# Queries and keys in 1 KB packets, and five chunks' probabilities turned on TensorE, in a windowed-attention and SoLU kernel

## The chip, the cores and the metric

The kernel runs on one core of one Trainium2 chip. The metric is the device time of one execution in microseconds. A core has TensorE (PE in the rows; PEld is its weight load), VectorE (DVE), ScalarE (ACT), GpSimd (POOL) and SyncE (SP), which here issues every DMA. Matmul results land in PSUM, all other tiles lie in SBUF; "DRAM" below is the chip's large memory behind the DMA queues.

## What is computed

Attention with a window and sink keys, and behind it a two-layer network with a SoLU in between, all in float32 (the weights arrive as float64):

```python
# q, k, v: (4, 8, 768, 64); n_sink = 4, window = 128
scores = (1 / sqrt(64)) * q @ k.T
keep = (key < n_sink) | ((0 <= query - key) & (query - key < window))
a = softmax(where(keep, scores, -1e9))
x = (a @ v).transpose(0, 2, 1, 3).reshape(3072, 512)
h = x @ w_in                                   # w_in: (512, 1024)
solu = h * softmax(h)
ln = (solu - mean(solu)) / sqrt(var(solu) + 1e-6) * g_ln
out = ln @ w_out                               # w_out: (1024, 512)
```

## The kernel before

The 4 x 768 tokens are 24 chunks of 128. `places` numbers them: chunk 0 is the first of batch 0, chunk 1 the first of batch 1, chunks 2 to 6 the rest of batch 0, 7 to 11 the rest of batch 1, 12 to 17 batch 2, 18 to 23 batch 3. Each chunk goes through the same stages:

- *Loading.* Queries and keys of chunks 0 to 6 come one chunk at a time (line 470) and are turned by TensorE against an identity (`turn`, line 513), which ScalarE copies out of PSUM (544, 548). For the other chunks a whole batch comes at once, in four DMAs each for q and k (line 473); VectorE turns them in 32x32 blocks (`turn_q` 526, `turn_keys` 539; `again_k` turns chunk 1's keys anew). The tiles `qn` and `kn` of such a batch have one buffer, so the next batch can't come before the last transpose of this one.
- *Scores* (567, TensorE) into one of two pairs of PSUM banks (`banks`, handed out by `claim` and given back by `done`), `pick` (584), masks with the row minimum (597, VectorE), exponentials (606, ScalarE), the inverse of the row sums (611, 612).
- *Normalising* (617, GpSimd) into `pn`, which has one buffer.
- *Turning the probabilities.* `pn` is stored to DRAM (`pd`; lines 632, 634, 637), reloaded in four pieces (`pb`, 642), and turned by VectorE in 32x32 blocks into `pt` (`flip_p`, 647). For chunks that are not the first of their batch, GpSimd splits `pt` into the part for the own and the part for the previous chunk's values (655, 661); sinks go a way of their own (667 to 694).
- *Values* (704, TensorE), x split into a high and a low part (709 ScalarE, 713 VectorE), *hidden layer* (724, three matmuls per block: high by high, high by low, low by high), SoLU and norm (729 to 764), a store and reload of u through DRAM and a turn on VectorE (771 to 781; chunks 0, 1, 22 and 23 are turned by TensorE, 790), split (797, 801), *projection* (815), scaling (821), store (826).

The two weights are made ready in the first part of the run: 16 blocks (`wraw`, line 373) are fetched as float64 and split into high and low parts by ScalarE, VectorE and TensorE (385 to 428).

Each step (a function with a chunk and an index) has a number, and the table `ORDER` (lines 19 to 118) says in which order the steps are issued. Each engine, and SP's DMA queue, runs its own instructions in just that order, and waits at the head of its queue. So the table sets what stands in front of what on every engine.

The lines that load a batch, take its raw tile and turn it:

```python
src[b, 2 * i:2 * i + 2].rearrange("h (t p) d -> p (h t) d", p=32)                          # 473
st[nm + "n", b].rearrange("p (e t x) -> p e t x", e=2, x=D)[:, :, 4 * c:4 * c + 4]         # raw
nc.vector.transpose(t[:, 2 * e:2 * e + 2], raw(n, "q")[:, e].rearrange("p t (y x) -> p y t x", y=2))
```

So partition p gets every 32nd row of a head, a piece of 64 floats (256 bytes) each.

Of the kernel before, what the change touches and what calls it, by code (L numbers as in the profile page):

```python
# [122 lines left out]
BIT_TAGS = ("uh", "ul", "ob", "uh", "ul", "ob", "uh", "ul") * 2  # L123
P = 128
NPS = 12
NSK = 4
W2P = 4
SEG = 132
BLK = 68
HALF = 64  # L130
NEG = 8.0e9
EPS_SUM = 1e-9
EPS_LN = 1e-6


# [48 lines left out]
def _banded(ctx, tc, q, k, v, n_sink, window, w_in, w_out, g_ln, out, val, wts, wpool, consts):  # L184
# [320 lines left out]
    def raw(n, nm):  # L505
        b, c = place(n)
        return st[nm + "n", b].rearrange("p (e t x) -> p e t x", e=2, x=D)[:, :, 4 * c:4 * c + 4]
# [530 lines left out]
```

## Time and profile before

| | |
|---|---|
| median of 3 runs | 436.63 us (435.45 to 438.84) |
| the profiled execution, its own time | 437.73 us |
| its span in the trace | 436.0 us |
| TensorE busy | 393.3 us (90%) |
| VectorE busy | 303.0 us (69%) |
| ScalarE busy | 249.5 us (57%) |
| GpSimd busy | 160.6 us (37%) |
| DMA | 81.45 MB in 118107 packets, 83228 of them under 512 B |

The shares of busy time are averages over a start in which weights and attention are made ready, a middle, and a long stretch in which little but the two layers is left; they hide that the engines take turns at being full. A busy time counts the union of an engine's instructions. Matmuls overlap in the pipeline, so their mean duration is longer than the distance of their starts. The DMA share adds the times of all packets over 16 engines and can pass 1 where packets of one engine overlap. The granted clock (PEclk) is the share of TensorE's full clock in a stretch.

### The profile page before, as it was taken

To read this page: it belongs to the slowest core of one execution; us is meant where nothing else is said; L and a number is where in the kernel's file an instruction comes from. 1 tells how busy PE (TensorE), PEld (TensorE's weight loads), DVE (VectorE), ACT (ScalarE), POOL (GpSimd) and SP (SyncE) were. 2 spreads that over 40 slices of the span, in tenths; PEclk is the share of its full clock that TensorE was granted. 3 is DMA by queue.
4 is the path that set the end of the run, shared out by engine and by line. 5 is a ranking of instruction groups with operands and counts; after the bars stand their busy time and mean duration, and the time that the engine had idled before them with its cause. 6 is when DMAs were issued, how large, how long until landed. Compare 5 with 4: busy or idle time off the path is not lost.

```text
span 436.0 us, 9545 instructions
## 1 busy us (share of the span) xinstructions
PE 393.3 (90%) x3347; PEld 306.5 (70%) x3347; DVE 303.0 (69%) x852; ACT 249.5 (57%) x688; POOL 160.6 (37%) x312
## 2 busy tenths in 40 slices
PE   2687899599997799998887999999999999999996
PEld 1353676478875588876665888888888887788875
DVE  5789899579975899847466667896764782736330
ACT  3788796466765567734635564655646653624351
POOL 5511253145552646333520131655431170605020
PEclk9999999879998999999996999999999999999999
DMA  8989999998999978499996438476539836263011
GB/s 224 270 254 241 255 239 197 184 225 220 261 176 230 278 211 247 140 235 240 174 238 216 141 97 253 112 234 170 169 111 234 209 100 195 75 190 98 2 73 55
DMA packets 118107, 81.45 MB, mean 187 GB/s; under 512 B 83228, under 2 KB 106148, under 8 KB 118052
## 3 DMA queue, kind: packets, MB, share of 16 engines
q1 hardware_dynamic: 118052, 80.77, 76.4%
q8 instruction: 28, 0.46, 0.5%
q14 instruction: 27, 0.22, 0.2%
HBM read 51.38 MB, written 29.49 MB: 185 GB/s over the span
## 4 chain that ended last, share of the span: by engine, by line
PE 62%; DMA 12%; SPq 10%; DVE 6%; ACT 4%; issue 3%; POOL 3%; DVEq 0%; POOLq 0%; ACTq 0%
PE o L815 27%; PE h L724 21%; PE av L704 7%; PE banks L567 4%; DMA pb<-pd 4%; SPq L473 3%; DMA wraw<-in_moe_w_in_dram 3%; SPq L642 2%; DMA pd<-pn 2%; POOL pn L617 2%; DMA ub<-ud 1%; DMA wraw<-in_moe_w_out_dram 1%; SPq L637 1%; PE av L694 1%; ACT sc L606 1%
## 5 line engine op out<-in xcount | busy, mean ns | idle before, releaser
L815 PE MATMUL o<-w2h,uh 128*128 128x512 f32 (+1 forms) x200 | 80.5, 402 | 4.3 <-ACT ob L821 4.3
L815 PE MATMUL o<-w2l,uh 128*128 128x512 f32 (+1 forms) x200 | 78.7, 394 | 5.3 <-DVE w2l L428 5.3
L606 ACT ACTIVATE sc<-sc,nmx 128x132 f32<-128x132 f32 x192 | 75.4, 396 | 12.8 <-DVE nmx L597 9.6
L617 POOL TENSOR_TENSOR pn<-sc,rs 128x512 f32<-128x512 f32 x48 | 51.9, 1092 | 75.2 <-DVE rs L612 30.1
L724 PE MATMUL h<-w1h,xh 128*128 128x512 f32 x192 | 77.7, 405 | 1.8 <-ACT w1l L426 0.7
L815 PE MATMUL o<-w2h,ul 128*128 128x512 f32 (+1 forms) x200 | 78.8, 394 | 0.4 <-DVE ul L801 0.2
L724 PE MATMUL h<-w1h,xl 128*128 128x512 f32 x192 | 75.8, 395 | 0.1
L724 PE MATMUL h<-w1l,xh 128*128 128x512 f32 x192 | 75.3, 392 | 0.0
L734 ACT ACTIVATE e<-h,nm 128x1024 f32<-128x1024 f32 x24 | 26.7, 1114 | 51.2 <-DVE nm L729 51.2
L655 POOL TENSOR_SCALAR_AFFINE_SELECT pc<-pt 128x512 f32<-128x512 f32 x40 | 28.0, 705 | 76.0 <-DVE pt L647 75.8
L597 DVE CUSTOM_DVE_ANT_0 sc<-banks,bias 128x132 f32<-128x132 f32 x192 | 47.4, 285 | 4.6 <-PE banks L567 1.0
L815 PEld LDWEIGHTS o<-w2h,uh 128*128 128x128 f32 x200 | 38.2, 191 | 15.7 <-ACT ob L821 4.8
L815 PEld LDWEIGHTS o<-w2l,uh 128*128 128x128 f32 x200 | 38.4, 192 | 13.7 <-DVE w2l L428 6.2
L797 ACT CAST uh<-ur 128x512 fp32r<-128x512 f32 x40 | 24.5, 615 | 37.0 <-DVE ur L781 32.2
L724 PEld LDWEIGHTS h<-w1h,xh 128*128 128x128 f32 x192 | 36.1, 188 | 13.5 <-issue 1.7
L815 PEld LDWEIGHTS o<-w2h,ul 128*128 128x128 f32 x200 | 38.3, 192 | 9.5 <-DVE ul L801 1.2
L647 DVE STREAM_TRANSPOSE pt<-pb 128x1024 f32<-128x1024 f32 x24 | 29.7, 1236 | 20.1 <-DMA pb<-pd 13.6
L567 PE MATMUL banks<-keys,q 32*64 32x200 f32 (+3 forms) x1280 | 38.4, 343 | 5.6 <-DVE nmx L597 5.6
L724 PEld LDWEIGHTS h<-w1h,xl 128*128 128x128 f32 x192 | 36.1, 188 | 9.4 <-DVE xl L713 1.3
L729 DVE TENSOR_REDUCE nm<-h 128x1 f32<-128x1024 f32 x24 | 29.2, 1218 | 17.3 <-PE h L724 17.0
L724 PEld LDWEIGHTS h<-w1l,xh 128*128 128x128 f32 x192 | 36.2, 188 | 6.8
L567 PEld LDWEIGHTS banks<-keys,q 32*64 32x64 f32 (+1 forms) x1280 | 29.2, 139 | 15.1 <-DVE nmx L597 5.7
(138 smaller groups left out, 682.4 us busy)
## 6 DMA issues: line engine op xcount, KB each, us to landing
pb<-pd SPq DMA_DIRECT2D x96, 128.0 KB, 3.7
ud<-u SPq DMA_DIRECT2D x20, 512.0 KB, 4.3
ub<-ud SPq DMA_DIRECT2D x80, 128.0 KB, 3.4
vn<-in_v_dram SPq DMA_DIRECT2D x24, 256.0 KB, 5.2
out_dram<-ob SPq DMA_DIRECT2D x23, 256.0 KB, 2.8
pd<-pn SPq DMA_DIRECT2D x40, 128.0 KB, 3.7
pd<-pn SPq DMA_DIRECT2D x20, 256.0 KB, 4.0
qn<-in_q_dram SPq DMA_DIRECT2D x12, 384.0 KB, 6.7
```

Of the source, the lines that this page charges most:

```text
L567: nc.tensor.matmul(st["s", n, g][ROWS[y], x, 256 * j + at:256 * j + at + wide], st["q", n][rows, m, ROWS[y]], kk[rows, m].rearrange("p b x ...
L597: nc.vector.tensor_tensor_reduce(out=st["sc", n][:, h], in0=st["s", n, g][:, x, 256 * j + BLK:256 * j + BLK + SEG], in1=bias0 if c == 0 el ...
L606: nc.scalar.activation(sc[:, h], sc[:, h], AF.Exp, bias=nmx[:, h:h + 1], scale=-1.0, accum_out=ssum[:, h:h + 1])
L617: nc.gpsimd.tensor_tensor(st["pn", n][:, 2 * i:2 * i + 2].rearrange("p b h x -> p h b x"), st["sc", n][:, :, PARTS[i]].rearrange("p h (b x ...
L647: nc.vector.transpose(pt.rearrange("p h (c t) -> p h c t", t=32), st["pb", n].rearrange("p c (h f) -> p h c f", f=32))
L655: nc.gpsimd.affine_select(st["pc", n][:, hs], st["pt", n][:, hs], pattern=[[0, HB], [1, P]], compare_op=ALU.is_ge, fill=0.0, base=0, chann ...
L704: nc.tensor.matmul(acc[ROWS[x], r, :], vals[:, 2 * r + x, :], p[:, 2 * r + x, :], start=alone, stop=alone or (r, i) == (NPAIR - 1, 1))
L724: nc.tensor.matmul(st["h", n][:, cols], a[:, kt, :], w[:, kt, cols], start=(kt == 0 and m == 0), stop=(kt == KT1 - 1 and m == 2))
L729: nc.vector.tensor_reduce(nm, st["h", n], axis=AX.X, op=ALU.max, negate=True)
L734: nc.scalar.activation(e, st["h", n], AF.Exp, bias=st["nm", n], scale=1.0, accum_out=se)
L797: nc.scalar.copy(uh, turned_u(n, g4))
L815: nc.tensor.matmul(st["o", n, i], a[:, kt % 4, :], part(w, kt)[:, i * wide:(i + 1) * wide], start=(kt == 0 and m == 0), stop=(kt == KT2 - ...
```

## The change

Four things change.

1. **Packets.** The batch loads (line 473) take four consecutive rows of a head as one piece: `h (c p r) d -> p (h c) (r d)` with r = `RUN` = 4, pieces of 256 floats (1 KB) in place of 64. Bytes, and the number of DMAs, stay. Within a chunk partition p now holds rows 4p to 4p + 3.
2. **Transposes.** A 32x32 transpose of one r therefore yields every fourth column. The outputs are written with a stride of four floats: `"p y (t r) -> p y r t"` for queries (two instructions a chunk of 256 elements, as before), `"p b (t r) -> p r b t"` for keys (four of 128 elements in place of two of 256).
3. **Probabilities.** For chunks 0 to 4 (`by_array`) the way through DRAM is gone: no store, no reload, no flip. `normalise` writes `pn` as head by key; `turn_p` multiplies each 64x64 quarter by a quarter of the identity on TensorE (32 matmuls a chunk) into a pair of PSUM banks claimed under the name `p`, with the own and previous halves put where the old layout had them; `take_p` copies it to `pt` on ScalarE, two instructions of 128x512 a chunk.
4. **Order.** `ORDER` is written anew from end to end.

```diff
+RUN = 4
...
-        nc.sync.dma_start(t.rearrange("p (m d) -> p m d", d=D)[32 * i:32 * (i + 1)],
-                          src[b, 2 * i:2 * i + 2].rearrange("h (t p) d -> p (h t) d", p=32))
+        nc.sync.dma_start(t.rearrange("p (m x) -> p m x", x=RUN * D)[32 * i:32 * (i + 1)],
+                          src[b, 2 * i:2 * i + 2].rearrange("h (c p r) d -> p (h c) (r d)", p=32, r=RUN))
...
-        return st[nm + "n", b].rearrange("p (e t x) -> p e t x", e=2, x=D)[:, :, 4 * c:4 * c + 4]
+        return st[nm + "n", b].rearrange("p (e c r y x) -> p e c y r x", e=2, c=NC, y=2, x=32)[:, :, c]
...
-                nc.vector.transpose(t[:, 2 * e:2 * e + 2], raw(n, "q")[:, e].rearrange("p t (y x) -> p y t x", y=2))
+                nc.vector.transpose(t[:, 2 * e:2 * e + 2].rearrange("p y (t r) -> p y r t", r=RUN), raw(n, "q")[:, e])
...
-        for e in range(2):
-            nc.vector.transpose(out[:, 2 * e:2 * e + 2, :, 0:HALF],
-                                raw(n, "k")[:, e].rearrange("p t (y x) -> p y t x", y=2))
+        for m in range(NPAIR):
+            nc.vector.transpose(out[:, m, :, 0:HALF].rearrange("p b (t r) -> p r b t", r=RUN), raw(n, "k")[:, m // 2, m % 2])
...
+    def by_array(n):
+        return n < 5
+
     def normalise(n, i):
+        if by_array(n):
+            if ("pn", n) not in st:
+                st["pn", n] = sb.tile([P, H, P], F32, tag="pn", name=f"pn_{n}", bufs=1)
+            nc.gpsimd.tensor_tensor(st["pn", n][:, :, ROWS[i]], st["sc", n][:, :, PARTS[i]],
+                                    st["rs", n].unsqueeze(2).to_broadcast([P, H, HALF]), op=ALU.mult)
+            return
...
+    def turn_p(n, j):
+        t = pair("p", n).rearrange("p y (h t) -> p y h t", t=HALF)
+        old = place(n)[1] > 0
+        for h in (2 * j, 2 * j + 1):
+            for y in range(2):
+                for i in range(2):
+                    nc.tensor.matmul(t[ROWS[i ^ 1 if old and y == 0 else i], y, h], st["pn", n][ROWS[y], h, ROWS[i]],
+                                     ident[ROWS[y], ROWS[y]], start=True, stop=True)
+
+    def take_p(n, y):
+        if ("pt", n) not in st:
+            st["pt", n] = sb.tile([P, H, P], F32, tag="pt", name=f"pt_{n}", bufs=2)
+        nc.scalar.copy(st["pt", n][:, :, ROWS[y]], pair("p", n)[:, y].rearrange("p (h t) -> p h t", t=HALF))
+        done("p", n)
...
-        invert: 1, normalise: 2, scale_sinks: later(1), store_p: lambda n: 3 if place(n)[1] > 0 else 1, load_p: 4, flip_p: 1,
+        invert: 1, normalise: 2, scale_sinks: later(1), store_p: lambda n: 0 if by_array(n) else 3 if place(n)[1] > 0 else 1,
+        load_p: lambda n: 4 * (not by_array(n)), flip_p: lambda n: int(not by_array(n)),
+        turn_p: lambda n: H // 2 * by_array(n), take_p: lambda n: 2 * by_array(n),
```

What the new order looks like at three places. In SP's DMA queue, where the last block of the second weight has been issued and the first whole batch (`qn_1`, `kn_1`) begins, the rows of before are

```order
L373 DMA wraw_14_856<-in_moe_w_out_dram 128x1024
L473 DMA qn_1_858<-in_q_dram 32x48x64
L642 DMA pb_3_905<-pd_3_813 32x4x256
L473 DMA kn_1_971<-in_k_dram 32x48x64 x3
L473 DMA qn_1_858<-in_q_dram 32x48x64
L642 DMA pb_3_905<-pd_3_813 32x4x256 x3
L637 DMA pd_4_1003<-pn_4_843 64x512
L473 DMA qn_1_858<-in_q_dram 32x48x64
L485 DMA vn_3_1011<-in_v_dram 128x8x64
L637 DMA pd_4_1003<-pn_4_843 64x512
```

and of the change

```order
L373 DMA wraw_13_893<-in_moe_w_out_dram 128x1024
L373 DMA wraw_12_898<-in_moe_w_out_dram 128x1024
L470 DMA qn_0_182<-in_q_dram 128x8x64
L470 DMA kn_0_136<-in_k_dram 128x8x64
L485 DMA vn_3_984<-in_v_dram 128x8x64
L473 DMA qn_1_1035<-in_q_dram 32x12x256 x2
L473 DMA kn_1_1051<-in_k_dram 32x12x256
L473 DMA qn_1_1035<-in_q_dram 32x12x256
L473 DMA kn_1_1051<-in_k_dram 32x12x256 x2
L473 DMA qn_1_1035<-in_q_dram 32x12x256
L485 DMA vn_4_1101<-in_v_dram 128x8x64
L473 DMA kn_1_1051<-in_k_dram 32x12x256
```

Before, stores and reloads of chunks 3 and 4 stand between the batch's loads; now the first store of probabilities is chunk 5's, and it stands behind the whole batch (its sizes are 32x12x256 where they were 32x48x64).

On VectorE, where chunk 7's query and the first keys of that batch are turned, the rows of before are

```order
L539 STREAM_TRANSPOSE keys_122<-kn_1_971 128x2x2x64 x4
L526 STREAM_TRANSPOSE q_7_1141<-qn_1_858 128x256 x2
L683 TENSOR_TENSOR skt_4_1144<-skp_4_1121,mine_119 128x512
L647 STREAM_TRANSPOSE pt_4_1148<-pb_4_1133 128x1024
L539 STREAM_TRANSPOSE keys_122<-kn_1_971 128x2x2x64 x2
```

and of the change

```order
L736 TENSOR_TENSOR xl_3_1191<-av_3_1088,xh_3_1189 128x512
L526 STREAM_TRANSPOSE q_7_1193<-qn_1_1035 128x2x4x32 x2
L399 SCALAR_TENSOR_TENSOR wbits_13_895<-wraw_13_893,wbits_13_895 128x512
L539 STREAM_TRANSPOSE keys_122<-kn_1_1051 128x4x2x16 x8
L610 TENSOR_SCALAR rs_6_1216<-ssum_6_1031 128x8
L611 RECIPROCAL rs_6_1216<-rs_6_1216 128x8
```

The flip of chunk 4 (`pt_4`) is gone, six key transposes that came in a group of four and one of two are eight smaller ones in a row, and weight blocks still stand around them (`wbits_13`).

On TensorE, in the early part where the scores of chunk 2 are made (`q_2`; `ws` belongs to the first weight, `banks` with `kn` or `qn` are transposes of loaded chunks), the rows of before are

```order
L513 MATMUL banks_0_86<-ident_88,qn_0_177 128x128 x4
L407 MATMUL ws_1_354<-wbits_1_218,minus_184 128x512
L421 MATMUL ws_1_354<-w1h_62,ident_r_93 128x512
L513 MATMUL banks_0_86<-ident_88,kn_0_134 128x128 x4
L567 MATMUL banks_1_87<-keys_122,q_2_345 64x200 x8
L567 MATMUL banks_0_86<-keys_122,q_2_345 64x200 x8
L407 MATMUL ws_4_405<-wbits_4_226,minus_184 128x512
```

and of the change

```order
L664 MATMUL banks_0_86<-ident_88,pn_0_266 64x64 x24
L566 MATMUL banks_1_87<-keys_122,q_2_319 64x200 x8
L664 MATMUL banks_0_86<-ident_88,pn_0_266 64x64 x8
L407 MATMUL ws_2_390<-wbits_2_347,minus_126 128x512
L421 MATMUL ws_2_390<-w1h_62,ident_r_93 128x512
L566 MATMUL banks_1_87<-keys_122,q_2_319 64x200 x8
L407 MATMUL ws_1_409<-wbits_1_270,minus_126 128x512
```

The 32 quarter turns of chunk 0 (`pn_0`, 64x64) stand before and between the two halves of chunk 2's scores.

Counted over the whole order of each engine: up to the low part of chunk 8's x (line 713 for that chunk) VectorE has 335 instructions before, without the reads of accumulators, and 364 after: flips 9 and 5, query transposes 20 and 18, key transposes 22 and 44, masks one chunk's 8 more, picks 22 and 25, inversions (611, 612) 13 and 14; all others as before. TensorE up to chunk 8's first hidden matmul has 160 quarter turns more, the scores of one chunk (32) and one sink transpose more; all others as before. SP issues 31 DMAs less.

## Rows read from the trace of the kernel before

**Rows 1.** The page's chain of work that ended last, as shares of the span by engine (SPq is SP's queue).

```profile
PE 62%; DMA 12%; SPq 10%; DVE 6%; ACT 4%; issue 3%; POOL 3%; DVEq 0%; POOLq 0%; ACTq 0%
```

**Rows 2.** Busy time of each engine by stretch: start and end, length, then busy us and number of instructions of PE, PEld, DVE, ACT and POOL; the granted clock of TensorE, the DMA share, and the rate in GB/s.

```profile
0.00:20.00 20.00, 7.69 (x54) 4.75 (x55) 12.64 (x47) 10.77 (x28) 11.93 (x45) 1.00 0.88 242
20.00:70.00 50.00, 42.53 (x344) 28.41 (x346) 46.79 (x132) 42.49 (x124) 15.71 (x23) 0.97 0.97 248
70.00:80.00 10.00, 10.00 (x89) 7.37 (x83) 8.20 (x36) 7.77 (x24) 1.04 (x2) 1.00 1.35 164
80.00:90.00 10.00, 5.59 (x29) 4.07 (x29) 5.80 (x11) 2.61 (x8) 3.67 (x5) 0.74 1.16 206
90.00:130.00 40.00, 39.87 (x475) 31.34 (x473) 35.09 (x122) 27.20 (x86) 19.94 (x37) 0.98 1.10 221
130.00:150.00 20.00, 14.74 (x178) 11.15 (x174) 13.28 (x49) 11.37 (x42) 8.11 (x14) 0.91 1.11 254
150.00:169.00 19.00, 18.91 (x244) 15.25 (x244) 18.09 (x63) 10.05 (x29) 11.21 (x21) 1.00 0.77 225
190.00:210.00 20.00, 18.52 (x162) 14.69 (x161) 11.99 (x38) 8.50 (x32) 9.27 (x18) 1.00 1.16 223
210.00:220.00 10.00, 7.19 (x113) 5.71 (x112) 4.03 (x5) 6.31 (x16) 5.25 (x12) 1.00 1.33 185
220.00:230.00 10.00, 8.85 (x37) 6.25 (x35) 5.64 (x22) 1.46 (x3) 3.70 (x6) 1.00 1.02 252
230.00:240.00 10.00, 7.32 (x94) 5.75 (x96) 7.25 (x19) 5.52 (x15) 0.00 (x0) 0.66 0.64 197
240.00:360.00 120.00, 120.00 (x958) 96.99 (x955) 85.31 (x216) 69.30 (x182) 46.55 (x86) 1.00 0.60 166
```

**Rows 3.** Instructions of TensorE in order of time, from three places (start us, length us of the group): scores of a 64x64 form and value products of the early part, then the scores and the first hidden matmuls of chunk 8 at 169 us.

```profile
12.83 1.29 PE L567 MATMUL banks<-keys,q 64*64 64x132 f32 x32
...
39.30 1.09 PE L704 MATMUL av<-pt,vn 128*64 128x128 f32 x16 [1.19 <-DVE pt L647]
...
167.46 1.61 PE L567 MATMUL banks<-keys,q 32*64 32x200 f32 x64
169.00 0.50 PE L724 MATMUL h<-w1h,xh 128*128 128x512 f32 x1
169.34 0.40 PE L724 MATMUL h<-w1l,xh 128*128 128x512 f32 x1
```

**Rows 4.** The chain of waits from 60 to 90 us, followed back from 90, in order of time (start us, length us, what).

```profile
69.58 1.67 SPq L473
...
71.30 2.55 SPq L473
...
73.89 2.32 SPq L473
...
79.26 4.34 DMA pb<-pd
```

**Rows 5.** The same chain, from 205 to 235 us.

```profile
211.25 4.04 SPq L473
...
223.78 6.06 DMA ub<-ud
```

**Rows 6.** VectorE's waits from 20 to 169 us: who waited for whom, us in total, times, longest.

```profile
DVE pt L647 <- DMA pb<-pd: 7.8, 3, 5.2
DVE keys L539 <- DMA kn<-in_k_dram: 2.8, 1, 2.8
DVE xl L713 <- ACT xh L709: 1.8, 1, 1.8
DVE q L526 <- issue: 1.8, 1, 1.8
DVE pt L647 <- issue: 1.3, 1, 1.3
```

**Rows 7.** DMA issues by line: destination and source, count, KB each, median us from issue to landing.

```profile
pb<-pd SPq DMA_DIRECT2D x96, 128.0 KB, 3.7
...
pd<-pn SPq DMA_DIRECT2D x40, 128.0 KB, 3.7
pd<-pn SPq DMA_DIRECT2D x20, 256.0 KB, 4.0
qn<-in_q_dram SPq DMA_DIRECT2D x12, 384.0 KB, 6.7
```

**Rows 8.** Groups of instructions, shapes kept apart: line, engine, operation, output and inputs, shapes and count; then busy us and mean ns of one; then idle time before them and what ended it.

```profile
L597 DVE CUSTOM_DVE_ANT_0 sc<-banks,bias 128x132 f32<-128x132 f32 x192 | 47.4, 285 | 4.6 <-PE banks L567 1.0 <-POOL sn L624 0.9
...
L647 DVE STREAM_TRANSPOSE pt<-pb 128x1024 f32<-128x1024 f32 x24 | 29.7, 1236 | 20.1 <-DMA pb<-pd 13.6 <-issue 6.4
...
L584 DVE COPY_PREDICATED banks<-m_old,banks 128x256 f32<-128x256 int32 x40 | 16.4, 422 | 1.8 <-PE banks L567 1.7
L597 DVE DVE_READ_ACCUMULATOR2_ANT nmx<- 128x1 f32 x192 | 15.8, 83 | 0.0
...
L539 DVE STREAM_TRANSPOSE keys<-kn 128x256 f32<-128x256 f32 x36 | 13.4, 414 | 5.1 <-DMA kn<-in_k_dram 2.8 <-issue 2.3
...
L544 ACT COPY q<-banks 128x512 f32<-128x512 f32 x7 | 4.1, 579 | 2.8 <-PE banks L513 2.5 <-DVE nmx L597 0.3
...
L555 POOL COPY keys<-keys 128x160 f32<-128x160 f32 x4 | 1.8, 453 | 3.8 <-DVE keys L539 3.7
```

195 rows, old and new, of the table ORDER are left out of this document.

## Prediction

> **What bounds the kernel now.** I read the views from the coarse to the fine. The page's chain of waits gives TensorE 62% of the span and DMA with its queue 22% [rows 1], so there are two limits and the question is where each holds. The table by stretch says where [rows 2]. From 240 to 360 us TensorE is busy for all 120 us: there only less TensorE work would help. Before that it is not: 7.69 of the first 20, 42.53 of the next 50, 5.59 of the ten from 80, 14.74 of the twenty from 130, and 8.1 us are idle from 190 to 240. To 169.0 us, where TensorE begins the hidden layer of chunk 8 [rows 3], its busy times add up to 139.3 us, so it idled 29.7.
>
> What else is full there? The DMA share is 0.88 or more in every stretch to 150 us, over 1 from 70 us on. And its rate falls where queries and keys of a batch come in: 164 GB/s from 70 to 80 us and 185 from 210 to 220, against 248 from 20 to 70 [rows 2]. The chain of waits shows what that does [rows 4]: from 69 us the queue is held by issues at line 473 (for 1.67, 2.55 and 2.32 us), and a reload of probabilities behind them lands after 4.34 us, at 83.6; VectorE's flip waits for it. At 211 to 230 us the chain runs alike, there from an issue of 4.04 us to a reload of u that takes 6.06 [rows 5].
>
> VectorE is nearly full too: 46.79 of 50 us from 20 to 70, 35.09 of 40 from 90 to 130, 18.09 of 19 from 150 [rows 2]. Its seven busy times to 169 us add up to 139.9, so 29.1 us are idle. Of these 7.4 lie in the first 20 us, before data is there. Of the rest the waits of VectorE from 20 to 169 us put 7.8 on the reload, 2.8 on the keys, and 1.8 and 1.3 on "issue" before the queries' transpose and the flip, both of which consume a DMA [rows 6]: 13.7 us in all that end with a transfer. So up to chunk 8 the order of limits is DMA, then VectorE, then TensorE; after 240 us it is TensorE alone. I therefore work out when VectorE has the low part of chunk 8's x, and add TensorE's remainder.
>
> **The change, part by part.** *DMA.* A later chunk's probabilities are stored in 2 x 128 + 256 KB and reloaded in 4 x 128 KB [rows 7], an early one's in the same bytes: 1.05 MB a chunk, 5.24 MB for five. At the 248 GB/s of 20 to 70 us [rows 2] that is 21 us of the queue, all before chunk 8, and 31 issues less on SP. The queries of a batch are 4 x 384 KB [rows 7], the keys as much, together 3.15 MB: 19.2 us at the 164 GB/s of the stretch that they fill, 12.7 at 248, so 6.5 us a batch, of which two lie before chunk 8. The queue gets some 34 us of air where transfers cost VectorE 13.7, so I take all of the 13.7 away. What is late next is VectorE's own work.
>
> *VectorE.* By the two orders, up to the low part of chunk 8's x it now does 4 flips less (1236 ns each: -4.9 us), 2 query transposes less (as large as the keys' of 414: -0.8), 44 key transposes of 128 elements for 22 of 256, and one chunk's masks (8 of 285 + 83 ns), 3 picks (422) and an inversion (0.4) more, +4.6. A flip of 1024 elements takes 1236 ns and a transpose of 256 takes 414 [rows 8], so 1.07 ns an element, and one of 128 is 414 - 137 = 277 ns: 44 x 0.277 - 22 x 0.414 = +3.1. The sum is +2.0 us, as long as an element costs what it does now.
>
> That is not known. The new transposes write each row's elements 16 bytes apart. Up to chunk 8 these are 18 x 256 + 44 x 128 = 10,240 elements a partition. Lower end: 0 more, by the row of the same operation on the same engine (L539) [rows 8]. A gain is excluded: bytes and elements are the same. Upper end: the only row that writes scattered pieces of 16 bytes, GpSimd's copy of sinks (L555), takes 453 ns for 160 elements [rows 8], 2.83 ns each, so 1.76 more than 1.07: 18.0 us. The nearer row is L539's; I go a third of the way, 0.55 ns: +5.6 us. [...]
>
> *TensorE.* A chunk's 32 quarter matmuls are 64 records (line 567 has 64 records for its 32 [rows 3]). Upper end, by the value product, 16 records in 1.09 us: 4.4 us a chunk. Lower end, by 64x64 quarters of 132 columns, 32 records in 1.29 us, taken by columns: 1.3. I take 1.6, the 64 records of a score [rows 3]: 8 us for five. Up to chunk 8 TensorE then has 139.3 + 8 + 1.6 (one chunk's scores stand earlier in its order) = 148.9 us of busy time, and 12.3 idle ones in the first 20 us [rows 2], which the change leaves alone: 161.2. So the quarters hide in TensorE's waiting for VectorE, but barely; the cover is a little larger than that, since the 139.3 hold stretched pieces (5.59 us at a granted 0.74 [rows 2], and the first matmul of a run is 0.50 us long where the next one starts 0.34 us behind it [rows 3]). Without the cover, if VectorE had x earlier, they would cost their 8 us in full, and the dearest ones 175 - 163 = 12 us even so: 433 us at the end.
>
> *ScalarE and GpSimd.* Ten copies of 128x512 out of PSUM at 579 ns [rows 8], 5.8 us, against ScalarE's 112 us of work in the first 169 [rows 2]: hidden. A quarter turn waits for GpSimd's normalised tile, and behind it in TensorE's queue stand the next chunk's scores; the wait replaces store, reload and flip, 3.7 + 3.7 + 1.2 us by their rows [rows 7, 8], so the path from sums to values gets shorter. Normalising keeps its element count.
>
> *To chunk 8:* 169.0 - 13.7 + 2.0 + 5.6 = 162.9 us.
>
> *After chunk 8.* Before, 436.0 - 169.0 = 267.0 us remain. 1.6 go for the scores that stand earlier. [...] The remainder is 257.4, and the span 162.9 + 257.4 = 420.3 us.
>
> The profiled execution took 437.73 us for a span of 436.0, 1.7 more; the median of the runs, 436.63, is 1.1 under it. So 420.3 + 1.7 - 1.1 = 420.9: **421 us**.
>
> **The rivals.** [...]
>
> *Each strided element takes a second step:* 1.07 ns more, 11.0 us instead of 5.6: 426.3 us. [...]
>
> *The transfers were hidden anyway:* VectorE is so full that the end of a DMA wait only lets it run into the next wait, for ScalarE or TensorE; the 1.8 us on ScalarE's high part of x [rows 6] are such a wait. [...] Against it: VectorE ran 50 us with 3.2 of idleness from 20 to 70 us, so its order can keep it fed.
>
> *Slower:* the strided write takes four steps an element, 3.2 ns more: 32.9 us of VectorE before chunk 8, 157.3 + 32.9 + 257.4 + 0.6 = 448.2 us. It decides from (436.6 - 415.3) / 10,240 = 2.1 ns more an element on. For it: nothing in the trace excludes it; against it, even GpSimd's scattered copy stays at 1.76.
>
> **How the numbers follow.** A measurement of this kernel can tell about 1% from no change, so faster is under 432.3 and slower over 441.0. Chances: the forecast 0.50 (its own range 415 to 427), better 0.18, the second step 0.12, hidden anyway 0.13, slower 0.07. The range has to leave out 0.20, which are the last two: 407 (the better case, 5 lower for a shorter start) to 434 (the 433.3 of the upper end of the stride). Faster: the first three and 0.03 of the hidden case, 0.83; same 0.10; slower 0.07.
>
> **What the new profile would show.** Right: DMA share well under 1 after 60 us; no wait of VectorE for reloads before 150 us worth more than 2 us; chunk 8's hidden layer beginning near 163 us; TensorE without idle stretches from there to the end but for the last 15 us; key transposes near 0.35 us and query transposes near 0.55 us. Wrong: key transposes over 0.5 us (stride), VectorE's idle time to chunk 8 above 20 us with ScalarE, TensorE or GpSimd as releasers (hidden anyway), quarter turns over 4.4 us a chunk or a TensorE that is full before chunk 8, or the idle stretch of the third load in its old size. The forecast fails most easily at the third of the way that I chose for the stride, and at the 13.7 us taken as a whole.

## The result and the profile after

The changed kernel takes 423.49 us (median of 4 runs, 422.02 to 424.8) against 437.74 for the kernel before beside it: ratio 0.967, 95% interval 0.959 to 0.974. Run again beside the experiments it took 424.69, ratio 0.966 (0.961 to 0.971). It is faster by 3.3 to 3.4%, 14 us; the forecast was 421. The profiled execution took 424.8 us and has a span of 423.1 us. The page's chain of waits, the line that answers to [rows 1]:

```profile
PE 57%; DMA 17%; DVE 17%; issue 3%; POOL 2%; ACT 2%; SPq 2%; DVEq 0%; POOLq 0%; ACTq 0%
```

The queue's share fell from 10% to 2%; VectorE's rose from 6% to 17%. These shares differ between executions: the profile of the second run has 6% and 14%. The table by stretch, columns as in [rows 2]:

```profile
0.00:20.00 20.00, 7.37 (x51) 5.52 (x52) 9.74 (x39) 9.36 (x28) 13.97 (x47) 1.00 0.90 245
20.00:70.00 50.00, 45.03 (x579) 29.83 (x579) 43.98 (x136) 44.81 (x128) 12.13 (x15) 1.00 0.64 178
70.00:80.00 10.00, 10.00 (x118) 7.80 (x122) 9.69 (x39) 10.00 (x32) 4.45 (x7) 1.00 1.13 208
80.00:90.00 10.00, 10.00 (x121) 8.51 (x112) 7.63 (x23) 9.23 (x24) 2.36 (x3) 1.00 0.88 173
90.00:130.00 40.00, 36.64 (x511) 28.56 (x510) 39.02 (x142) 24.93 (x88) 23.02 (x45) 1.00 0.91 212
130.00:150.00 20.00, 17.79 (x210) 13.93 (x209) 15.93 (x64) 12.60 (x44) 9.26 (x16) 0.91 0.92 223
150.00:169.00 19.00, 19.00 (x221) 14.95 (x218) 18.57 (x62) 11.84 (x39) 10.05 (x17) 1.00 0.95 253
169.00:190.00 21.00, 20.73 (x255) 16.60 (x255) 17.65 (x61) 14.03 (x47) 12.71 (x22) 1.00 1.05 233
190.00:210.00 20.00, 18.16 (x160) 14.02 (x157) 17.57 (x61) 11.69 (x35) 5.73 (x10) 1.00 0.97 221
210.00:240.00 30.00, 30.00 (x295) 24.37 (x295) 25.07 (x67) 18.91 (x52) 13.76 (x26) 1.00 0.68 207
240.00:360.00 120.00, 119.95 (x830) 96.22 (x828) 75.77 (x168) 61.06 (x146) 42.10 (x81) 1.00 0.59 164
```

Three things are to be seen. From 20 to 70 us the DMA share fell from 0.97 to 0.64 [rows 2]: the reloads of five chunks are gone. From 70 to 80 us, where queries and keys of a batch are loaded, all transfers together now move 208 GB/s, where they moved 164 [rows 2]. And TensorE is busy for all of 70 to 90 us, where it had 5.59 of ten before, and for all of 210 to 240, where it idled 6.64 [rows 2]. Where chunk 8's hidden layer begins, in TensorE's instructions in order of time (start, length), as in [rows 3]:

```profile
167.35 0.45 PE L747 MATMUL h<-w1h,xh 128*128 128x512 f32 x1
```

It begins at 167.35 us, where 162.9 was forecast and 169.0 was the value before. From there to the end are 255.8 us (forecast 257.4, before 267.0). So the sum was nearly right, but its first half was not: up to chunk 8 came 1.7 of the 6.1 us, behind it 11.2 instead of 9.6. In the profile of the second run (span 424.8 us) it begins at 166.70 us: 2.3 us up to there and 8.9 behind.

Up to chunk 8 TensorE's busy times in the table add up to 144.2 us (19.00 of the stretch from 150 counted to 167.35), 4.9 more than before; it idled 23.2 instead of 29.7. Behind chunk 8 it idled 1.84 us from 190 to 240 instead of 8.1 [rows 2]; in the second run's profile 3.4.

VectorE's waits from 20 to 169 us, as in [rows 6]:

```profile
DVE q L526 <- DMA qn<-in_q_dram: 3.8, 2, 3.4
DVE sc L596 <- PE banks L566: 3.6, 1, 3.6
DVE banks L583 <- PE banks L566: 1.4, 3, 0.7
DVE ul L824 <- ACT uh L820: 1.2, 1, 1.2
DVE keys L539 <- DMA kn<-in_k_dram: 1.2, 1, 1.2
```

The waits for reloads (7.8 in [rows 6]) are gone; waits for TensorE's scores (3.6 + 1.4) and for queries have come. VectorE's busy times to 169 us add up to 144.6 us, so 24.4 are idle, against 29.1 before. In the first 20 us 10.3 are idle, where it was 7.4; from 20 us on 14.2, where it was 21.8. The groups that the change touches, columns as in [rows 8]:

```profile
L539 DVE STREAM_TRANSPOSE keys<-kn 128x128 f32<-128x128 f32 x72 | 19.8, 396 | 2.2 <-DMA kn<-in_k_dram 2.2
L526 DVE STREAM_TRANSPOSE q<-qn 128x256 f32<-128x256 f32 x34 | 18.9, 633 | 5.0 <-DMA qn<-in_q_dram 3.8 <-DMA pb<-pd 1.2
...
L664 PE MATMUL banks<-ident,pn 64*64 64x64 f32 x320 | 6.0, 221 | 0.0
```

The five chunks' quarters take TensorE 6.0 us, 1.2 a chunk. Of the transposes the busy time is used here, not the mean: 72 times 396 ns would be 28.5 us, but the group is busy for 19.8, since neighbours overlap in the records.

### The profile page after: what moved, and what is told of

Same layout as the page of the kernel before. It is cut to its first block, busy times and chain, and to the rows that moved or that the text cites. A ratio compares the mean times of both kernels' runs of the same rounds, so it can differ in the third digit from the quotient of the medians.

```text
span 423.1 us, 10174 instructions
## 1 busy us (share of the span) xinstructions
PE 393.6 (93%) x3667; PEld 309.1 (73%) x3667; DVE 304.5 (72%) x883; ACT 253.9 (60%) x698; POOL 159.7 (38%) x312
## 4 chain that ended last, share of the span: by engine, by line
PE 57%; DMA 17%; DVE 17%; issue 3%; POOL 2%; ACT 2%; SPq 2%; DVEq 0%; POOLq 0%; ACTq 0%
PE o L838 23%; PE h L747 20%; DMA qn<-in_q_dram 7%; PE av L727 6%; PE banks L566 5%; DMA kn<-in_k_dram 3%; DVE sc L596 3%; DVE keys L539 3%; DMA pd<-pn 3%; DMA ub<-ud 2%; PE banks L513 1%; DVE pt L655 1%; DVE banks L583 1%; DMA pb<-pd 1%; DMA out_dram<-ob 1%
## 5 line engine op out<-in xcount | busy, mean ns | idle before, releaser
L838 PE MATMUL o<-w2h,uh 128*128 128x512 f32 (+1 forms) x200 | 79.2, 396 | 0.5 <-DVE xl L736 0.5
L838 PE MATMUL o<-w2h,ul 128*128 128x512 f32 (+1 forms) x200 | 77.7, 388 | 0.2
L838 PE MATMUL o<-w2l,uh 128*128 128x512 f32 (+1 forms) x200 | 77.6, 388 | 0.0
L625 POOL TENSOR_TENSOR pn<-sc,rs 128x512 f32<-128x512 f32 x38 | 39.6, 1050 | 47.0 <-DMA pd<-pn 22.2
L678 POOL TENSOR_SCALAR_AFFINE_SELECT pc<-pt 128x512 f32<-128x512 f32 x40 | 26.1, 663 | 68.8 <-DVE pt L655 59.4
L838 PEld LDWEIGHTS o<-w2h,uh 128*128 128x128 f32 x200 | 37.8, 189 | 10.5 <-issue 1.6
L747 PEld LDWEIGHTS h<-w1h,xh 128*128 128x128 f32 x192 | 36.2, 188 | 12.3 <-issue 3.0
L752 DVE TENSOR_REDUCE nm<-h 128x1 f32<-128x1024 f32 x24 | 29.1, 1212 | 21.7 <-PE h L747 21.6
L824 DVE TENSOR_TENSOR ul<-ur,uh 128x512 fp32r<-128x512 f32 x40 | 30.0, 755 | 14.0 <-ACT uh L820 13.8
L762 DVE SCALAR_TENSOR_TENSOR u<-h,e 128x1024 f32<-128x1024 f32 x24 | 29.3, 1220 | 12.3 <-ACT e L757 12.3
```

The lines of the kernel that those rows point to most:

```text
L625: nc.gpsimd.tensor_tensor(st["pn", n][:, 2 * i:2 * i + 2].rearrange("p b h x -> p h b x"), st["sc", n][:, :, PARTS[i]].rearrange("p h (b x ...
L678: nc.gpsimd.affine_select(st["pc", n][:, hs], st["pt", n][:, hs], pattern=[[0, HB], [1, P]], compare_op=ALU.is_ge, fill=0.0, base=0, chann ...
L747: nc.tensor.matmul(st["h", n][:, cols], a[:, kt, :], w[:, kt, cols], start=(kt == 0 and m == 0), stop=(kt == KT1 - 1 and m == 2))
L752: nc.vector.tensor_reduce(nm, st["h", n], axis=AX.X, op=ALU.max, negate=True)
L762: nc.vector.scalar_tensor_tensor(u, st["h", n], -1.0 / DFF, st["e", n], op0=ALU.mult, op1=ALU.mult, accum_out=nmu)
L824: nc.vector.tensor_tensor(ul, turned_u(n, g4), st["uh", n, g4].bitcast(F32), op=ALU.subtract)
```

## The experiments

P stands for the 1 KB packets with strided transposes, A for the quarter turns. Each kernel was timed beside the kernel before; its ratio is to that one. The diffs are shortened to the lines, or parts of lines, that carry the edit.

### Each part without the other

P alone in the kernel before, that is the change's lines of the load, `raw`, `turn_q` and `turn_keys`:

```diff
-"h (t p) d -> p (h t) d", p=32
+"h (c p r) d -> p (h c) (r d)", p=32, r=RUN
...
```

> The kernel before with the 1 KB packets and the strided transposes alone; probabilities go through DRAM as before, the order of the steps is that of before. Theory of the forecast (transfers hold VectorE up): VectorE pays about 9 us for the stride up to chunk 8 (10,240 elements at the 0.9 ns that the trace after shows), and the waits for keys, queries and reloads shrink by at most 13.7; the idle stretch of TensorE from 190 to 240 us, 8.1 us, shrinks to under 4: 426 to 435 us. Rival (the new order of the steps does it): the stride is paid and nothing comes back, 438 to 446 us, and the idle stretch after 190 us keeps its size.

Measured: 428.34 us, ratio 0.976 (0.973 to 0.979): most of the gain, in the old order. Table by stretch:

```profile
80.00:90.00 10.00, 6.92 (x45) 4.93 (x45) 6.03 (x11) 3.73 (x14) 3.90 (x5) 0.83 1.13 230
...
210.00:240.00 30.00, 26.11 (x229) 20.54 (x224) 24.42 (x72) 15.44 (x39) 6.27 (x12) 1.00 0.87 230
```

TensorE's hole at 80 us is smaller by 1.3 us than in [rows 2], the one behind 210 by 2.7. The time lies in the range of the forecast's theory, and the rival that the order does it all is out.

The opposite, the changed kernel without P:

```diff
-"h (c p r) d -> p (h c) (r d)", p=32, r=RUN
+"h (t p) d -> p (h t) d", p=32
...
```

> The changed kernel with 256-byte packets and contiguous transposes; quarter turns and the new order stay. Theory of the forecast: the stride's 9 us up to chunk 8 come back, the slow loads return before chunk 8 (up to 6.5 us a batch) and in the third load (up to 8 us): 422 to 430 us. Rival (the packets cost VectorE more than they save): 412 to 419 us, faster than the changed kernel. Second rival (the packets carry most of the gain): 431 to 438 us.

Measured: 436.35 us, ratio 0.993 (0.990 to 0.996). The second rival: without P nearly all is gone. Table by stretch:

```profile
70.00:80.00 10.00, 10.00 (x111) 7.78 (x114) 9.70 (x38) 10.00 (x32) 4.45 (x7) 1.00 1.38 170
...
130.00:150.00 20.00, 14.98 (x170) 11.56 (x151) 11.31 (x48) 9.19 (x30) 8.81 (x17) 0.83 1.16 210
...
190.00:210.00 20.00, 15.18 (x166) 12.25 (x165) 8.55 (x33) 8.45 (x31) 5.30 (x11) 0.91 1.24 181
210.00:240.00 30.00, 29.49 (x254) 23.12 (x253) 27.26 (x78) 20.03 (x59) 10.35 (x18) 1.00 0.76 207
```

To 70 us this kernel runs like the changed one; then the slow load comes in at 170 GB/s (208 there), and TensorE loses 2.8 us more from 130 to 150 and 3.0 more from 190 to 210 (1.6 against the second run's profile), at a lower granted clock (0.83 and 0.91, where the changed kernel has 0.91 and 1.00). VectorE's transposes stand idle longer before they begin:

```profile
L539 DVE STREAM_TRANSPOSE keys<-kn 128x256 f32<-128x256 f32 x36 | 13.6, 417 | 3.7 <-DMA kn<-in_k_dram 3.7
L526 DVE STREAM_TRANSPOSE q<-qn 128x256 f32<-128x256 f32 x34 | 12.9, 417 | 10.9 <-DMA vo<-in_v_dram 6.0 <-DMA qn<-in_q_dram 4.1 <-DMA pb<-pd 0.8
```

They wait 14.6 us (3.7 + 10.9), where the changed kernel waits 7.2 (2.2 + 5.0), for transfers in both. What P shortens is a load for which the program waits. Chunk 8's hidden layer begins at 173.97 us here and at 165.93 with P alone; the changed kernel begins it at 167.35, the kernel before at 169.00 [rows 3]:

```profile
173.97 0.45 PE L748 MATMUL h<-w1h,xh 128*128 128x512 f32 x1
```

```profile
165.93 0.51 PE L724 MATMUL h<-w1h,xh 128*128 128x512 f32 x1
```

So with A and the new order alone chunk 8 comes 4.9 us later than before, and it is P that brings it forward. Behind chunk 8, 260.5 us remain without P (span 434.5), 261.1 with P alone (span 427.0) and 255.8 with everything, against 267.0 before: there P gains, and so do A and the order. One chunk's scores, 1.6 us by the forecast, are only moved by the order, from behind chunk 8 to ahead of it.

Both parts in the order of before (chunks 0 to 4 alike, each at a place where a PSUM bank is free):

```diff
-store_p(3, 2)
+turn_p(3, 0), turn_p(3, 1), turn_p(3, 2), turn_p(3, 3), take_p(3, 0), take_p(3, 1)
...
-store_p(3, 1), store_p(3, 0), load_p(3, 1), load_p(3, 0), load_p(3, 2), load_p(3, 3), flip_p(3, 0)
```

> Both parts, 1 KB packets and quarter turns, in the order of before: each early chunk's six new steps stand in one piece where its store or its reload stood. Theory of the forecast: within 5 us of the changed kernel, 421 to 429 us. Rival (the new order of the steps does it): 432 to 442 us.

Measured: 437.93 us, ratio 0.996 (0.994 to 0.999), in the rival's range: placed like this the quarters cost 9.6 us over P alone. From this kernel to the changed one only the order differs, and that is worth 13 us. Table by stretch, then SP's waits from 40 to 90 us:

```profile
70.00:80.00 10.00, 7.27 (x94) 5.79 (x94) 5.56 (x10) 6.21 (x22) 4.52 (x8) 0.83 0.01 2
```

```profile
SPq L449 <- PE banks L489: 15.9, 2, 13.8
```

From 70 to 80 us the DMA engines do nothing: line 449 is the next batch's load, which waits 13.8 us for TensorE's transposes (line 489) to free its buffer. Air in the queue is of no use while the load behind it has no buffer.

The changed kernel without A:

```diff
-        return n < 5
+        return n < 0
...
-turn_p(3, 0), turn_p(3, 2), turn_p(3, 1), turn_p(3, 3), take_p(3, 0), take_p(3, 1)
+store_p(3, 2), store_p(3, 1), store_p(3, 0), load_p(3, 0), load_p(3, 1), load_p(3, 2), load_p(3, 3), flip_p(3, 0)
```

> The changed kernel with the five first chunks' probabilities through DRAM again: the stores right behind the normalising, the reloads where the quarter turns and their first copy stood, the flip in place of the last copy or just ahead of the first reader; 1 KB packets and the rest of the new order stay. Theory of the forecast: VectorE gets five flips (6.2 us) and waits for reloads (up to 7.8 us) back, so 431 to 438 us. Rival (the order and the packets do it, the reload was hidden): 422 to 427 us.

Measured: 445.24 us, ratio 1.013 (1.010 to 1.017), slower than either theory said. Table by stretch, then the longest of SP's waits from 10 to 100 us:

```profile
20.00:70.00 50.00, 36.90 (x253) 21.62 (x252) 38.41 (x116) 33.70 (x93) 6.74 (x9) 0.86 0.86 225
...
80.00:90.00 10.00, 4.00 (x25) 2.55 (x25) 5.61 (x19) 5.04 (x17) 1.00 (x2) 0.57 0.95 242
```

```profile
SPq L616 <- POOL pn L601: 14.1, 2, 7.5
```

TensorE is busy 8.1 us less from 20 to 70 than in the changed kernel. But 4.8 of these are the quarter turns themselves, which only the changed kernel has there (its line 664 alone):

```profile
20.00:70.00 50.00, 4.82 (x256) 4.32 (x256) 1.00 0.64 178
```

So 3.3 us are lost to 70 us. From 80 to 90 us 6.0 are missing, of which at most 1.2 are quarters. The stores (line 616) hold SP's queue for 14.1 us until GpSimd has normalised, with the next loads behind them. Both runs depend on where I put the steps, so A and the order are not priced apart. Shown is that A did not pay in the order of before, and that the new order is bad without it, each with the steps placed as here.

### Does VectorE set the pace?

The same 1 KB packets, but contiguous writes:

```diff
-t[:, 2 * e:2 * e + 2].rearrange("p y (t r) -> p y r t", r=RUN)
+t[:, 2 * e:2 * e + 2].rearrange("p y (r t) -> p y r t", r=RUN)
...
-out[:, m, :, 0:HALF].rearrange("p b (t r) -> p r b t", r=RUN)
+out[:, m, :, 0:HALF].rearrange("p b (r t) -> p r b t", r=RUN)
```

> The changed kernel with the same 1 KB packets, but the transposes write their 32 (queries) or 16 (keys) elements of a row one behind the other. So the columns of later queries and keys stand in another order than the masks take them, and the output of the chunks behind the first batch is not the reference's; count and sizes of all instructions are unchanged. Theory of the forecast (the stride costs VectorE, and VectorE sets the time to chunk 8): query transposes at 411 ns, key transposes at 277, 9 us less VectorE work up to chunk 8 and 5 to 9 us less in the end: 414 to 419 us. Rival (the stride's time fits into VectorE's waits): the transposes get as short, the end does not move: 421 to 425 us. Second rival (the stride is not what makes them long): transposes stay at 633 and 396 ns, 423 us.

Measured: 424.20 us, ratio 0.966 (0.962 to 0.971), as the changed kernel. The groups:

```profile
L539 DVE STREAM_TRANSPOSE keys<-kn 128x128 f32<-128x128 f32 x72 | 15.7, 277 | 3.4 <-DMA kn<-in_k_dram 3.4
L526 DVE STREAM_TRANSPOSE q<-qn 128x256 f32<-128x256 f32 x34 | 12.9, 418 | 4.7 <-DMA vo<-in_v_dram 3.7 <-DMA qn<-in_q_dram 1.0
```

The stride costs (19.8 - 15.7) + (18.9 - 12.9) = 10.1 us of VectorE in the whole program, over 72 x 128 + 34 x 256 = 17,920 elements: 0.56 ns an element. All of it fits into waits: the stride's time is not what sets the pace here. The same in the order of before:

> The order of before and the probabilities through DRAM, with 1 KB packets, and transposes that write their elements one behind the other, so that the columns of later queries and keys stand in another order than the masks take them and the output of the chunks behind the first batch is not the reference's. The forecast took VectorE for the next limit: with 9 us less VectorE work up to chunk 8 than with the stride, 418 to 423 us against 428 with it. Rival (VectorE's work fits into its waits in this order too): 426 to 429 us.

Measured: 427.48 us, ratio 0.970 (0.966 to 0.974) against 0.976 (0.973 to 0.979): about 2.5 us, a quarter of the 10.1 us of VectorE's time, with intervals that overlap. Whether the stride costs anything in the end there is not shown; the time lies in the rival's range.

### Packet size and stride

Pieces of two tokens: 512-byte packets, writes 8 bytes apart.

```diff
-RUN = 4
+RUN = 2
...
-"p (e c r y x) -> p e c y r x", e=2, c=NC, y=2, x=32
+"p (e c u r y x) -> p e c y u r x", e=2, c=NC, u=2, y=2, x=32
...
+                for y in range(2):
+                    nc.vector.transpose(t[:, 2 * e + y].rearrange("p (u t r) -> p u r t", u=2, r=RUN), raw(n, "q")[:, e, y])
```

> The changed kernel with pieces of two tokens: 512-byte packets, elements written 8 bytes apart instead of 16, a query transpose of 256 elements as two of 128. If a write costs more as soon as it is scattered: a transpose of 128 elements stays at 396 ns, VectorE gets 34 more of them for 34 of 633, +2.8 us up to chunk 8, loads between the two rates: 424 to 430 us. [...]

Measured: 427.57 us, ratio 0.973 (0.969 to 0.978). The groups, and the stretch of the load:

```profile
L540 DVE STREAM_TRANSPOSE keys<-kn 128x128 f32<-128x128 f32 x72 | 15.7, 279 | 3.7 <-DMA kn<-in_k_dram 3.7
L527 DVE STREAM_TRANSPOSE q<-qn 128x128 f32<-128x128 f32 x68 | 14.9, 278 | 6.7 <-DMA qn<-in_q_dram 6.7
```

```profile
70.00:80.00 10.00, 10.00 (x130) 7.81 (x129) 9.68 (x39) 10.00 (x33) 4.46 (x7) 1.00 1.22 195
```

The expected price, 396 ns for a transpose of 128 elements as soon as its writes are scattered, was wrong: 8 bytes apart costs nothing (279 ns as in the contiguous 277), 16 bytes apart takes 396. Yet VectorE's gain does not count, and the packets do: with 256, 512 and 1024 bytes all transfers together move 170, 195 and 208 GB/s from 70 to 80 us, and the ends are 436.35, 427.57 and 424.69. The kernel with contiguous writes shows it without the stride: its VectorE transposes cost about the same as those with 256 and 512 bytes (28.6 us against 26.5 and 30.6), and it ends at 424.20. The step from 512 to 1024 bytes is small: the intervals of the ratios overlap a little (0.969 to 0.978, 0.961 to 0.971).

### Are the quarter turns hidden?

```diff
+for _ in range(2):
     nc.tensor.matmul(t[...], st["pn", n][...], ident[...], start=True, stop=True)
```

> The changed kernel with each quarter matmul issued twice into the same place: 320 more records, 6 us more TensorE work, all before chunk 8. Theory of the forecast (the quarters lie in TensorE's waiting for VectorE): 0 to 2 us later, 423 to 426 us. Rival (TensorE is the limit there by now): 4 to 6 us later, 427 to 430 us.

Measured: 434.45 us, ratio 0.990 (0.985 to 0.994): 9.8 us later, more than even the rival said. The trace is of an execution of 439.46 us, the longest of six. TensorE's group, the stretch from 70 to 80, and the issues of the batch's queries from 55 to 100 us (shortest, median and longest in ns, then first and last start), there and in the changed kernel:

```profile
L665 PE MATMUL banks<-ident,pn 64*64 64x64 f32 x640 | 11.8, 222 | 3.5 <-issue 3.5
```

```profile
70.00:80.00 10.00, 10.00 (x210) 7.96 (x210) 8.99 (x31) 8.80 (x28) 3.12 (x7) 1.00 0.22 53
```

```profile
L473 SPq DMA_DIRECT2D qn<-in_q_dram x4: 348/462/469, 77.0 to 80.3; - x4
```

```profile
L473 SPq DMA_DIRECT2D qn<-in_q_dram x4: 348/462/469, 68.3 to 71.7; - x4
```

5.8 us more of TensorE work, and the load starts 8.7 us later: in both kernels SP's issue waits for TensorE's transposes (line 513) to free the buffer, 9.5 us in all, 9.0 the longest. More quarter work is not hidden: it stands ahead of the next load. What the first 6.0 us of it cost is not measured by itself.

### The single buffer

Two buffers of three chunks for the queries and keys of a batch, and three of two:

```diff
+piece(j): sb.tile([P, (NC // PIECES) * H * D], tag=f"{nm}{j}", bufs=1)
+for h in range(2):  # one head of one piece an issue
+    nc.sync.dma_start(piece(j)...[32 * g:32 * (g + 1), h], src[b, 2 * g + h, j * per * P:(j + 1) * per * P]...)
```

> The changed kernel with the queries and the keys of a batch in two buffers of three chunks each instead of one of six (same bytes in all, same 1 KB packets, one head and three chunks an issue, the first half issued first). So the first half's load needs to wait only for chunk 3's transposes, not for chunk 6's, and chunk 7 needs only the first half. Theory now (what is left of TensorE's waits between 85 and 170 us, 9.6 us, and from 190 to 210 us, 2 us, hangs on the single buffer): DMA share from 20 to 70 us rises over 0.64, the first load of queries is issued near 58 us instead of 68, and the end comes 4 to 10 us earlier: 414 to 420 us. Rival (those waits are VectorE's and ScalarE's own work in its order): within 2 us, 422 to 426 us. Second rival (32 small issues a batch instead of 8 slow the queue): 427 us or more.

> The same with three buffers of two chunks each, 48 issues a batch. By the theory now it lies within 3 us of the kernel with two buffers, 412 to 421 us; if the number of issues counts, it is slower than that one by 3 us or more.

Measured: 424.85 us, ratio 0.967 (0.963 to 0.971), and 440.14, ratio 1.003 (1.000 to 1.006). The kernel with two buffers ends in the range of its first rival, by which the waits are the engines' own work in their order. The one with three ends 15 us later, as the case that the number of issues counts had it. SP's waits from 20 to 130 us, in the changed kernel and with two buffers:

```profile
SPq L473 <- PE banks L513: 9.5, 2, 9.0
```

```profile
SPq L484 <- PE banks L579: 0.4, 1, 0.4
```

The wait for the buffer went, the end did not move. The issues from 55 to 100 us, of keys in the changed kernel and of both with two buffers, and the chain of waits with three (start, length, what):

```profile
L473 SPq DMA_DIRECT2D kn<-in_k_dram x4: 312/470/5029, 69.8 to 73.7; - x4
```

```profile
L484 SPq DMA_DIRECT2D qn<-in_q_dram x16: 312/428/1587, 59.3 to 77.3; - x16
L484 SPq DMA_DIRECT2D kn<-in_k_dram x16: 312/429/1938, 66.1 to 81.0; - x16
```

```profile
120.55 0.42 SPq L484
121.02 0.43 SPq L484
```

The first half leaves 9.0 us earlier (59.3 instead of 68.3), the last keys 7.3 later (81.0 instead of 73.7): with three buffers an issue takes the queue 0.47 us from one start to the next (120.55 and 121.02), so by an estimate from that 32 of them take at least 15 us a batch and 48 of them nearly 23. But with two buffers the late end of the load is not what VectorE waits for. Its groups, then its waits from 20 to 169 us:

```profile
L552 DVE STREAM_TRANSPOSE keys<-kn 128x128 f32<-128x128 f32 x72 | 19.8, 392 | 0.0
L539 DVE STREAM_TRANSPOSE q<-qn 128x256 f32<-128x256 f32 x34 | 18.8, 631 | 0.0
```

```profile
DVE sc L609 <- PE banks L579: 4.1, 1, 4.1
DVE banks L596 <- PE banks L579: 2.6, 3, 1.6
DVE sc L609 <- POOL pn L638: 2.2, 2, 2.0
```

The transposes' waits fell from 7.2 us to nothing, and VectorE waits for TensorE's scores (6.7 us instead of 5.0) and for GpSimd's normalising (2.2) instead. A load that comes earlier than in the changed kernel gains nothing as long as these stay as they are. What a second buffer would give without the many issues is open. The two buffers in the order of before, without quarters:

> The order of before and the probabilities through DRAM, with 1 KB packets, strided transposes and two buffers of three chunks each for the queries and the keys of a batch (the first half issued first, one head and three chunks an issue). Theory now (in this order a reload of probabilities behind the batch's load holds VectorE, and TensorE idles 3 us from 80 to 90 us; the quarter turns only bought that wait off for 6 us of TensorE work): the first half's load leaves earlier, the reload lands sooner, and the end comes at 419 to 425 us, as early as the changed kernel without any quarter turn. Rival (the loads come earlier, and the reloads queue behind them all the same): 427 to 433 us.

Measured: 434.92 us, ratio 0.990 (0.986 to 0.994), about 6 us later than with one buffer, and beyond even the rival's range. Whether this comes of the reloads behind the loads or of the time of the issues was not tried.

The changed kernel run again had this expectation, and met it (the numbers stand at the top):

> The changed kernel once more, beside the runs of before on the same chip, for a narrower ratio than its first: 0.959 to 0.974 of before, 420 to 427 us.

No version beat the changed kernel beyond the measurement.

## Why the prediction came out right

The forecast, 421 us, is met within 1%, in part by luck: it was 4.4 us too early up to chunk 8 and 1.6 us too long behind it, and these errors offset each other in part. The mechanism holds for the packets and for the second half, and fails for the first.

**The transfers as the first limit: right.** P alone gives 0.976, and the changed kernel without P falls back to 0.993. The faster the load of a batch, the earlier the end (170, 195 and 208 GB/s), until VectorE's transposes wait for it no more: their waits go from 14.6 us to 7.2 with P, and the end comes 12 us earlier; they go to 0.0 with two buffers, and the end stays.

**"I take all of the 13.7 away": wrong, the step that failed.** Of the 13.7 us that ended with a transfer, 5.0 are left, now waits for queries and keys (3.8 + 1.2). VectorE's whole idle time to 169 us shrank by 4.7 us, from 29.1 to 24.4, a third of the 13.7: that is the rival "hidden anyway", by which the end of one wait only lets VectorE run into the next. Of the idle time 7.4 us lay in the first 20 us before, and 10.3 do now. In place of the reloads VectorE waits for TensorE's scores and for queries. By the prediction's own mark for that rival (over 20 us idle, with TensorE among the releasers) the step is refuted. But the forecast's sum with a third of the 13.7 in place of all, 172.0 us (169.0 - 4.6 + 2.0 + 5.6), misses too: 167.35 lies halfway between it and the forecast's 162.9. And the way by which the wait was to go, the probabilities out of the queue, did not bring chunk 8 forward by itself: without P it begins at 173.97 us, 4.9 later than before, of which only 1.6 are the scores that stand earlier.

**"What is late next is VectorE's own work": wrong as far as the stride goes.** Contiguous writes took 10.1 us off VectorE and nothing off the time. TensorE is nearer to being next: busy without a gap from 70 to 90 us, and 5.8 us more of it cost 9.8. But it is not full either. It idles 10.5 us between 20 us and chunk 8, and its longest waits from 90 to 150 us are for VectorE's turn of the queries (2.2 us) and for the low part of u (1.8). The engines wait for each other in turn.

**The stride: right in size, of no effect.** 0.56 ns an element by busy time; 0.55 were taken. The 5.6 us were spent, but beside other waits. The price of the rival, 1.07 ns, is not reached in VectorE's time, though the mean lengths of single instructions come closer (633 - 418 ns for 256 elements, 396 - 277 for 128). Up to its own chunk 8, at 167.35 us, VectorE is busy for 142.9 us, 3.0 more than before, where the sum had 7.6.

**"8 us, hidden": the price nearly right, the cover missing.** 6.0 us instead of 8; doubled, they were not hidden. The prediction's own count (161.2 us for TensorE against 162.9) said "barely"; it took for granted that the 12.3 idle microseconds of the first 20 are the only ones that stay, and TensorE kept 23.2 up to chunk 8.

**The new order: no term of its own.** The sum gives it 1.6 us for scores that stand earlier. Between both parts in the order of before and the changed kernel lie 13 us, and which of the moved steps make them was not tried.

**After chunk 8: right, 255.8 for 257.4.** The 8.0 us that the sum takes off here beyond the 1.6 of the scores (267.0 - 1.6 - 257.4) were an estimate of mine, and no run shows that term by itself; in its place the profiles showed 9.6 (11.2 - 1.6) and, in the second run, 7.3 (8.9 - 1.6). Of the 11.2 us, 6.3 are idle time of TensorE from 190 to 240 us (8.1 before, 1.84 after), and its granted clock was 1.00 from 210 to 240 us, where the last ten had 0.66 [rows 2]. That the packets carry a good part is shown: without P 5.3 us are idle from 190 to 240 (4.82 + 0.51 in its table), with it 1.84 and, in the second run, 3.4.

Of the other signs that the prediction named, no wait for a reload before 150 us is over 2 us, as forecast. The DMA share is not well under 1 after 60 us (1.13 from 70 to 80 us, 1.05 from 169 to 190), and the transposes are longer one by one, 396 and 633 ns for 350 and 550.

So up to chunk 8 errors of both signs met in part: the stride and VectorE's other terms were charged in full and cost nothing that the end shows, while the 13.7 were gained in full and the quarters left out.

## What to carry to other kernels

Two engines that are both nearly full can both be next: before a wait is counted as gained, ask of the other engine whether it could have gone earlier, and of work put onto it whether it feeds the loads (here the transposes that free a buffer). Larger packets paid here where a load is waited for, even with dearer transposes (P alone: ratio 0.976); once nobody waited for it, an earlier load paid nothing (424.85 with two buffers, 424.69 with one). Fewer transfers did not pay while the next load had no buffer (437.93 us against 428.34 for P alone). Price short back-to-back instructions by the busy time of their group (19.8 us for the 72 key transposes) and not by the mean length of one (72 times 396 ns, 28.5 us).

## What the hardware showed beyond that

VectorE's 32x32 transposes write fp32 elements 8 bytes apart at the contiguous price (279 against 277 ns for 128 elements, 15.7 us for 72 both times), and 16 bytes apart at 396 ns (19.8 us for 72). Why the one costs nothing and the other does was not shown.

With packets of 512 bytes all transfers together moved 195 GB/s from 70 to 80 us, against 208 with 1 KB and 170 with 256 bytes. And issues of 64 KB in a row start 0.47 us apart on SP's queue; those of 96 KB are 0.43 us long by the median. The kernel with 48 issues a batch ended 15 us later than the one with 8 (440.14 against 424.69).
